# One value visit per head pair and a deeper weight ring in a fused attention, MLP and experts kernel

## The chip, the cores and the metric

The kernel runs on one core of one Trainium2 chip, as one launch. The metric is device time in microseconds, the median of three runs; the kernel before takes 1066.63 us (1066.08 to 1066.88). Durations below come from one profiled execution of the same kernel.

## The reference

Three layers follow each other on 1792 tokens (4 batches of 448): attention with a tanh cap on the scores, an MLP with a piecewise quadratic activation, and a layer of eight experts of which each token takes one. All inputs are f32, but for the two matrices of the first MLP, which arrive as f64. In short:

```python
def reference(q, k, v, cap, moe_w_in, moe_w_out, w_gate, w1, w2):
    # attention, 4 batches x 12 heads x 448 x 64
    scores = q @ k.T / sqrt(64)
    scores = cap * tanh(scores / cap)
    attn = exp(scores - max(scores)); attn /= sum(attn) + 1e-9
    x = concat_heads(attn @ v)                      # 1792 x 768
    # first MLP, 768 -> 2048 -> 768
    h = x @ moe_w_in
    g = where(h >= 1, h, where(h <= -1, 0, (h + 1)**2 / 4))
    x = g @ moe_w_out
    # experts, 8 of them, top 1
    e = argmax(x @ w_gate); p = softmax(x @ w_gate)[e]
    out = p * (relu(x @ w1[e]) @ w2[e])             # 768 -> 1024 -> 768
```

## The kernel before

**Arithmetic.** The large products keep f32 accuracy by splitting both operands into a high part that the fast f32 mode of TensorE (fp32r) holds exactly and a low rest. Each product is then three matmuls: high by high, low by high and high by low. The splits of the raw MLP weights are `unit_split` (ScalarE casts the high part, line 1287; VectorE subtracts for the low part, line 965). The products of probabilities with values (line 1133) and the sums of the probabilities (line 1137) are plain f32, which the profile shows as two records for each matmul.

**Attention.** Heads are handled in pairs, six to a batch, 24 in all, numbered g. For a pair, `load` and `load_v` fetch k, q and v, `prep` transposes k and q on TensorE into high and low parts, and `scores(g, c)` makes the transposed scores of a chunk c of keys: chunks 0 to 2 are 128 keys wide, for both heads, as a 128x896 tile whose matmuls use 64 rows of the array each; chunk 3 is the last 64 keys of both heads at once, through the block diagonal tile `kd`, 128x448, on the whole array. ScalarE applies tanh and exp to each chunk, and the result is the tile t of probabilities (tags pe and po for even and odd chunks, three tiles each, all of full size). `values(g, c)` adds the chunk's product with v into a PSUM tile, 64 columns of the array for each head; with chunk 3 go four matmuls for the sums, from chunk 3 and from `ta`, the sum of the other three chunks, made on VectorE. `finish` copies both out, inverts the sums by way of DRAM (den_s) and scales.

**First MLP.** For a batch, `gemm1` makes 16 column blocks of h from 32 units of weights (two units of 384 columns for each block, nine matmuls for each unit) and `gemm2` 6 blocks of y from 24 units of 512. `step(u)` asks for the raw weights of unit u+4 and for the split of unit u+2. Raw weights lie in a ring of three tiles (tag wr). In batch 0 the f64 weights are first converted to f32 and stored in DRAM (wi_s, wo_s); the units of all batches are read from there.

**The order.** Nothing runs where it is written. Every step is recorded with its engine, an estimated cost, its inputs and outputs, and a class `Plan` simulates the five engines and the transfers and emits each engine's instructions in the order of its simulated starts. A step starts when its inputs are done, its engine is free and its tiles have a free place; among several the one recorded earlier goes first, shifted by a table of numbers by name. A transfer is held back while the simulated backlog of the transfers is long. The engines then run these orders strictly. The generators `attn_gen` and `moe1_gen` record the steps: attention of batch b+1 beside the first MLP of batch b, so the attention of batches 1 to 3 lies beside the first MLP of batches 0 to 2. In `attn_gen`, u counts the chunks of a batch, and the values of chunk u - 2 (LAG) are recorded after the scores of chunk u. The experts come last, in an order written by hand.

Of the kernel before, what the change touches and what calls it, by code (L numbers as in the profile page):

```python
# [11 lines left out]
F32 = mybir.dt.float32  # L12
# [9 lines left out]
B, H, S, D = 4, 12, 448, 64  # L22
# [884 lines left out]
def kernel(ctx, tc, q, k, v, cap, w_in, w_out, w_gate, w1, w2, consts, cols, out):  # L907
# [136 lines left out]
    def load(g):  # L1044
        b, pr = divmod(g, NP)
        kq = A([CP, NCH, 4, D], F32, "kq", f"kq{g}", 1)
        for j in range(2):
            for a, i, order in ((k, j, "(c p) d -> p c d"), (q, 2 + j, "(p c) d -> p c d")):
                on, qe = ("ACT", ACT) if g == 0 and i > 1 else ("SP", SP)
                op(on, 630, lambda a=a, i=i, j=j, order=order, qe=qe: qe.dma_start(kq.t[:, :, i], a[b, 2 * pr + j].rearrange(order, c=NCH)),  # L1050
                   wr=[(kq, i)], dma=8 * S * D)
        st[g] = dict(kq=kq)
# [35 lines left out]
    def scores(g, c):  # L1088
# [21 lines left out]
        t = A([128, 2, S], F32, "po" if c % 2 else "pe", f"t{g}_{c}", 3)  # L1110
# [11 lines left out]
    def values(g, c):  # L1122

        s = st[g]
        if c == 0:
            s["pv"] = Sym(PA, [128, 512], F32, "pv", 1, f"pv{g}")
            s["su"] = Sym(PA, [128, 512], F32, "su", 1, f"su{g}")
        pvs, sus, t = s["pv"], s["su"], s["p", c]

        def go():  # L1130
            px = lambda j: t.t[:, j if c < 3 else 0]
            for j in range(2):
                PE.matmul(pvs.t[rows(j), :S], s["vn"][:, c, j], px(j), start=c == 0, stop=c == 3)  # L1133
            if c == 3:
                for n in range(4):
                    j, i = n // 2, n % 2
                    PE.matmul(sus.t[32 * n : 32 * n + 32, :S], one[:, (1 + j) * i], px(j) if i else s["ta"].t[:, j], start=True, stop=True)

        op("PE", 1740 if c == 3 else 870, go, rd=[(t, j) for j in range(2 if c < 3 else 1)] + [(s["vk"], i) for i in range(4)] + [("one", 0)]
           + ([(s["ta"], 0)] if c == 3 else []), wr=[(pvs, 0)] + ([(sus, 0)] if c == 3 else []), duty=0.87)  # L1140
# [28 lines left out]
    def attn_gen(b):  # L1169
# [12 lines left out]
        for u in range(4 * NP + LAG):  # L1182
# [4 lines left out]
            if u >= LAG:  # L1187
                done = b * NP + (u - LAG) // 4
                values(done, (u - LAG) % 4)
# [69 lines left out]
    def unit_load(u):  # L1259
# [6 lines left out]
        r = Sym(MP, [128, 512], F32, "wr", 3, f"wr{u}")  # L1266
# [24 lines left out]
    def step(u):  # L1291
        unit_load(u + 4)
        unit_split(u + 2)
# [3 lines left out]
    def gemm1(b):  # L1297
        u = b * NU
        if b == 0:
            for i in range(4):  # L1300
                unit_load(i)
# [369 lines left out]
```

## Time and profile before

| | |
|---|---|
| median of three runs | 1066.63 us (1066.08 to 1066.88) |
| the profiled execution: time, span | 1065.99 us, 1064.1 us |
| busy TensorE, weight load, VectorE, ScalarE, GpSimd | 95%, 73%, 49%, 49%, 13% |
| TensorE's mean granted clock | 0.985 of full speed |
| value matmuls (line 1133), 384 records | 96.4 us busy, 593 ns mean |
| transfers | 162.56 MB, mean 153 GB/s |

The busy time of a matmul is modelled and overlaps with its neighbours, so a duration of 0.37 us does not mean that the next matmul starts 0.37 us later. What a matmul costs in a stream is read from the distance of the starts. Attention of batch 0 lies between 7 and some 85 us, the first MLP of batch 0 begins at 84 us, and the last value visit of batch 3 is at 586.59 us. The last stretch, from some 760 us on, is the experts.

### The profile page before, as it was taken

The page shows a single profiled execution, that of the slowest core. Times are in us where ns is not written, and L with a number is a line of the kernel's source. Part 1 is how long each engine was busy: PE and PEld are TensorE (multiplying, and loading weights), DVE is VectorE, ACT ScalarE, POOL GpSimd, SP SyncE. Part 2 cuts the span into 40 slices and gives each one's busy share as a digit, 9 for nine tenths or more (in the row PEclk, how much of TensorE's full clock was granted, in tenths as well). Part 3 has the DMA queues.
Part 4 walks back from the last instruction along what each step waited for, and adds up shares of the span by engine and source line. Part 5 has one row for each costly group of instructions (what it writes and reads, how often), then busy time and mean ns, then how long its engine had stood idle before and what let it go on. Part 6 is the DMA issues. An engine that isn't in the chain of part 4 may idle for free. (4 is left out here: it accounts for less than half of the span.)

```text
span 1064.1 us, 17421 instructions
## 1 busy us (share of the span) xinstructions
PE 1010.5 (95%) x5546; PEld 778.6 (73%) x5546; DVE 522.0 (49%) x1054; ACT 525.4 (49%) x872; POOL 134.4 (13%) x199
## 2 busy tenths in 40 slices
PE   6978899999999999999999999999999989999995
PEld 3435677777687767876777888799767858888984
DVE  5878899678476643357653347752541101110110
ACT  5867667648656653557665344452521212222221
POOL 2221011011020101011101002000311111111110
PEclk9988899999999999999999999999999999999998
DMA  7778888888553444254342344772138883211111
GB/s 225 187 209 235 262 248 257 265 262 248 155 118 105 121 104 119 83 118 111 108 126 74 104 127 95 235 234 90 53 122 315 306 291 117 70 41 47 46 46 34
DMA packets 167809, 162.56 MB, mean 153 GB/s; under 512 B 90805, under 2 KB 139437, under 8 KB 167682
## 3 DMA queue, kind: packets, MB, share of 16 engines
q1 hardware_dynamic: 163202, 147.83, 47.3%
q0 software_dynamic: 3408, 13.00, 3.7%
q8 instruction: 56, 0.92, 0.4%
q14 instruction: 71, 0.58, 0.2%
q10 hardware_dynamic: 1072, 0.23, 0.1%
HBM read 190.39 MB, written 24.39 MB: 202 GB/s over the span
## 5 line engine op out<-in xcount | busy, mean ns | idle before, releaser
L965 DVE TENSOR_TENSOR wl<-wr,wh 128x384 fp32r<-128x384 f32 (+1 forms) x224 | 138.6, 622 | 116.9 <-ACT wh L1287 114.2
L1287 ACT CAST wh<-wr 128x384 fp32r<-128x384 f32 (+1 forms) x224 | 123.7, 557 | 118.4 <-PE y L1347 69.3
L1318 PE MATMUL h<-xh,wh 128*128 128x448 f32 x384 | 146.8, 382 | 2.1 <-DVE g L1327 1.9
L1320 PE MATMUL h<-xh,wl 128*128 128x448 f32 x384 | 142.5, 371 | 1.8 <-DVE wl L965 1.8
L1346 PE MATMUL y<-gh,wh 128*128 128x448 f32 x384 | 144.0, 375 | 0.0
L1319 PE MATMUL h<-xl,wh 128*128 128x448 f32 x384 | 141.9, 369 | 0.4 <-DVE xl L965 0.4
L1347 PE MATMUL y<-gl,wh 128*128 128x448 f32 x384 | 140.3, 365 | 0.0
L1348 PE MATMUL y<-gh,wl 128*128 128x448 f32 x384 | 140.3, 365 | 0.0
L1112 ACT ACTIVATE t<-sc,csc 128x896 f32<-128x896 f32 x96 | 86.8, 916 | 30.5 <-PE sc L1106 15.0
L1133 PE MATMUL pv<-t,vn 128*64 128x448 f32 x384 | 96.4, 593 | 5.0 <-DVE ev L1150 3.4
L499 DVE TENSOR_TENSOR hl<-ht,hh 128x512 fp32r<-128x512 f32 x26 | 18.0, 691 | 165.6 <-ACTq L598 159.9
L1318 PEld LDWEIGHTS h<-xh,wh 128*128 128x128 f32 x384 | 72.9, 190 | 32.5 <-issue 13.3
L1113 ACT ACTIVATE t<-t,capx 128x896 f32<-128x896 f32 x96 | 90.7, 954 | 1.8
L1346 PEld LDWEIGHTS y<-gh,wh 128*128 128x128 f32 x384 | 72.1, 188 | 23.2 <-issue 13.9
L1320 PEld LDWEIGHTS h<-xh,wl 128*128 128x128 f32 x384 | 72.9, 190 | 10.1 <-DVE wl L965 3.7
L1319 PEld LDWEIGHTS h<-xl,wh 128*128 128x128 f32 x384 | 73.0, 190 | 6.5 <-DVE xl L965 0.8
L511 PE MATMUL ey<-w2h,hh 128*128 128x384 f32 x208 | 74.5, 358 | 2.4 <-issue 2.4
L1348 PEld LDWEIGHTS y<-gh,wl 128*128 128x128 f32 x384 | 72.1, 188 | 5.9
L1347 PEld LDWEIGHTS y<-gl,wh 128*128 128x128 f32 x384 | 72.2, 188 | 5.3
L512 PE MATMUL ey<-w2l,hh 128*128 128x384 f32 x208 | 69.9, 336 | 0.0
L513 PE MATMUL ey<-w2h,hl 128*128 128x384 f32 x208 | 69.9, 336 | 0.0
L1325 ACT ACTIVATE g<-h,half 128x448 f32<-128x448 f32 x64 | 40.5, 635 | 53.5 <-PE h L1320 51.6
(252 smaller groups left out, 1617.0 us busy)
## 6 DMA issues: line engine op xcount, KB each, us to landing
s<-in_moe_w_dram SPq DMA_DIRECT2D x84, 512.0 KB
s<-in_moe_w_dram SPq DMA_DIRECT2D x104, 384.0 KB
wr<-wi_s SPq DMA_DIRECT2D x128, 192.0 KB
wr<-wo_s SPq DMA_DIRECT2D x96, 256.0 KB
raws<-in_moe_w_in_dram SPq DMA_DIRECT2D x12, 768.0 KB
raw<-in_moe_w_out_dram SPq DMA_DIRECT2D x12, 512.0 KB
wo_s<-cv SPq DMA_DIRECT2D x24, 256.0 KB
kq<-in_k_dram SPq DMA_DIRECT2D x48, 112.0 KB
```

The lines of the kernel that those rows point to most:

```text
L511: nc.tensor.matmul(o, hh[:, i], self.w2h[f][:, c], start=f == 0, stop=False)
L965: eng.tensor_sub(out, a, hi.bitcast(F32))
L1112: op("ACT", a_(n * S) + 35, lambda: ACT.activation(t.t[:, :n], pt.t[:, :n, :S], AF.Tanh, scale=csc), rd=[(pt, 0), ("cap", 0)], wr=all_)
L1113: op("ACT", a_(n * S) + 85, lambda: ACT.activation(t.t[:, :n], t.t[:, :n], AF.Exp, scale=capx), wr=all_)
L1133: PE.matmul(pvs.t[rows(j), :S], s["vn"][:, c, j], px(j), start=c == 0, stop=c == 3)
L1287: op("ACT", a_(n), lambda: ACT.copy(hi.t[:, :n], r.t[:, :n]), rd=[(r, 0)], wr=[(hi, 0)])
L1318: PE.matmul(pm.t[:, :S], part_of(hi, a), xh[b].t[:, i], start=i == 0, stop=False)
L1319: PE.matmul(pm.t[:, :S], part_of(hi, a), xl[b].t[:, i], start=False, stop=False)
L1320: PE.matmul(pm.t[:, :S], part_of(lo, a), xh[b].t[:, i], start=False, stop=i == NDC - 1)
L1346: PE.matmul(pm.t[:, :S], part_of(hi, f % 4), gh[b].t[:, f], start=f == 0, stop=False)
L1347: PE.matmul(pm.t[:, :S], part_of(hi, f % 4), gl[b].t[:, f], start=False, stop=False)
L1348: PE.matmul(pm.t[:, :S], part_of(lo, f % 4), gh[b].t[:, f], start=False, stop=f == NFC - 1)
```

## The change

Four things are changed. The probabilities of chunks 0 to 2 share one ring of six full tiles (tag p), and chunk 3 has two tiles of half the size (tag pc). In batches 1 to 3 the values of a pair are recorded once, with all four chunks and the sums, where chunk 3 was recorded before; batch 0 keeps a visit for each chunk. Raw weights of even units lie in three further tiles (tag wr2, in the attention's pool), so that there are six, except in the last batch, where the pool is gone; `step` asks for unit u+6, and `gemm1(0)` begins with six loads. The first pair's two q loads are issued on SP instead of ACT.

```diff
--- before.py
+++ after.py
@@ -1046,8 +1046,7 @@
         kq = A([CP, NCH, 4, D], F32, "kq", f"kq{g}", 1)
         for j in range(2):
             for a, i, order in ((k, j, "(c p) d -> p c d"), (q, 2 + j, "(p c) d -> p c d")):
-                on, qe = ("ACT", ACT) if g == 0 and i > 1 else ("SP", SP)
-                op(on, 630, lambda a=a, i=i, j=j, order=order, qe=qe: qe.dma_start(kq.t[:, :, i], a[b, 2 * pr + j].rearrange(order, c=NCH)),
+                op("SP", 630, lambda a=a, i=i, j=j, order=order: SP.dma_start(kq.t[:, :, i], a[b, 2 * pr + j].rearrange(order, c=NCH)),
                    wr=[(kq, i)], dma=8 * S * D)
         st[g] = dict(kq=kq)
 
@@ -1107,7 +1106,7 @@
 
         op("PE", scc(c), go, rd=[(x, 0) for x in (kh, kl, qh, ql)] + ([("kd", (i, h)) for i in range(2) for h in range(2)] if c == 3 else []),
            wr=[(pt, 0)], duty=0.8)
-        t = A([128, 2, S], F32, "po" if c % 2 else "pe", f"t{g}_{c}", 3)
+        t = A([128, 2, S], F32, "p", f"t{g}_{c}", 6) if c < 3 else A([128, 1, S], F32, "pc", f"t{g}_{c}")
         all_ = [(t, j) for j in range(n)]
         op("ACT", a_(n * S) + 35, lambda: ACT.activation(t.t[:, :n], pt.t[:, :n, :S], AF.Tanh, scale=csc), rd=[(pt, 0), ("cap", 0)], wr=all_)
         op("ACT", a_(n * S) + 85, lambda: ACT.activation(t.t[:, :n], t.t[:, :n], AF.Exp, scale=capx), wr=all_)
@@ -1119,25 +1118,27 @@
             ta = s["ta"]
             op("DVE", d1(2 * S), lambda: DVE.tensor_add(ta.t, ta.t, t.t), rd=all_, wr=[(ta, 0)])
 
-    def values(g, c):
+    def values(g, cs):
 
         s = st[g]
-        if c == 0:
+        if 0 in cs:
             s["pv"] = Sym(PA, [128, 512], F32, "pv", 1, f"pv{g}")
             s["su"] = Sym(PA, [128, 512], F32, "su", 1, f"su{g}")
-        pvs, sus, t = s["pv"], s["su"], s["p", c]
+        pvs, sus = s["pv"], s["su"]
+        ts = {c: s["p", c] for c in cs}
 
         def go():
-            px = lambda j: t.t[:, j if c < 3 else 0]
-            for j in range(2):
-                PE.matmul(pvs.t[rows(j), :S], s["vn"][:, c, j], px(j), start=c == 0, stop=c == 3)
-            if c == 3:
+            px = lambda c, j: ts[c].t[:, j if c < 3 else 0]
+            for c in cs:
+                for j in range(2):
+                    PE.matmul(pvs.t[rows(j), :S], s["vn"][:, c, j], px(c, j), start=c == 0, stop=c == 3)
+            if 3 in cs:
                 for n in range(4):
                     j, i = n // 2, n % 2
-                    PE.matmul(sus.t[32 * n : 32 * n + 32, :S], one[:, (1 + j) * i], px(j) if i else s["ta"].t[:, j], start=True, stop=True)
-
-        op("PE", 1740 if c == 3 else 870, go, rd=[(t, j) for j in range(2 if c < 3 else 1)] + [(s["vk"], i) for i in range(4)] + [("one", 0)]
-           + ([(s["ta"], 0)] if c == 3 else []), wr=[(pvs, 0)] + ([(sus, 0)] if c == 3 else []), duty=0.87)
+                    PE.matmul(sus.t[32 * n : 32 * n + 32, :S], one[:, (1 + j) * i], px(3, j) if i else s["ta"].t[:, j], start=True, stop=True)
+
+        op("PE", 870 * (len(cs) + (3 in cs)), go, rd=[(t, j) for c, t in ts.items() for j in range(2 if c < 3 else 1)] + [(s["vk"], i) for i in range(4)] + [("one", 0)]
+           + ([(s["ta"], 0)] if 3 in cs else []), wr=[(pvs, 0)] + ([(sus, 0)] if 3 in cs else []), duty=0.9)
 
     def finish(g):
         b, pr = divmod(g, NP)
@@ -1186,7 +1187,9 @@
                 yield scc(c)
             if u >= LAG:
                 done = b * NP + (u - LAG) // 4
-                values(done, (u - LAG) % 4)
+                c_ = (u - LAG) % 4
+                if b == 0 or c_ == 3:
+                    values(done, range(4) if b else (c_,))
                 if (u - LAG) % 4 == 3:
                     finish(done)
                     if done + 2 < B * NP:
@@ -1263,7 +1266,7 @@
         n = 384 if i < 2 * NFC else 512
         while b == 0 and words and conv_n[0] <= (i // 2 if i < 2 * NFC else i - NFC):
             conv_one(conv_n[0])
-        r = Sym(MP, [128, 512], F32, "wr", 3, f"wr{u}")
+        r = Sym(MP, [128, 512], F32, "wr", 3, f"wr{u}") if b == B - 1 or u % 2 else A([128, 512], F32, "wr2", f"wr{u}", 3)
         if words:
             src = wi_s[i] if i < 2 * NFC else wo_s[i - 2 * NFC]
             go = lambda: SP.dma_start(r.t[:, :n], src)
@@ -1289,7 +1292,7 @@
         wsp[u] = hi, lo
 
     def step(u):
-        unit_load(u + 4)
+        unit_load(u + 6)
         unit_split(u + 2)
 
     part_of = lambda s, i: s.t[:, i * 128 : i * 128 + 128]
@@ -1297,7 +1300,7 @@
     def gemm1(b):
         u = b * NU
         if b == 0:
-            for i in range(4):
+            for i in range(6):
                 unit_load(i)
             unit_split(0)
             unit_split(1)
```

What this does to the order on TensorE, in the second layer of batch 1's MLP beside the attention of batch 2. y is the MLP's second product, pt the transposes of `prep`, sc the scores, pv the values, su the sums; the first digit of a t is the chunk. Before:

```order
L1133 MATMUL pv_4290<-t_1_4220,vn_99 64x448 x2
L1078 MATMUL pt_1_4321<-ct,kq_4119 128x112 x4
L1103 MATMUL sc_3_4326<-qh_4117,kd 128x448 x2
L1103 MATMUL sc_3_4326<-ql_4131,kd 128x448
L1346 MATMUL y_2_4279<-gh_3138,wh_4200 128x448
...
L1133 MATMUL pv_4290<-t_2_4286,vn_99 64x448 x2
...
L1133 MATMUL pv_4290<-t_3_4342,vn_99 64x448 x2
L1137 MATMUL su_4381<-ta_4232,one 32x448
L1137 MATMUL su_4381<-t_3_4342,one 32x448
```

After, at the same pair (line numbers are now those of the new file):

```order
L1077 MATMUL pt_1_4327<-ct,kq_4127 128x112 x4
L1102 MATMUL sc_3_4336<-qh_4125,kd 128x448 x2
L1102 MATMUL sc_3_4336<-ql_4144,kd 128x448
L1349 MATMUL y_2_4285<-gh_3113,wh_4250 128x448
...
L1134 MATMUL pv_4371<-t_0_4190,vn_99 64x448 x2
L1134 MATMUL pv_4371<-t_1_4224,vn_99 64x448 x2
L1134 MATMUL pv_4371<-t_2_4292,vn_99 64x448 x2
L1134 MATMUL pv_4371<-t_3_4351,vn_99 64x448 x2
L1138 MATMUL su_4380<-ta_4229,one 32x448
L1138 MATMUL su_4380<-t_3_4351,one 32x448
```

The four chunks of values, which stood in four places with GEMM matmuls between them, stand in one, ahead of the sums, and behind 12 GEMM matmuls that follow the last scores.

On SP at the start of the program (kq holds k and q of a pair, raws the f64 weights, vn the values). Before:

```order
L935 DMA ct<-in_consts_dram 128x393
L1050 DMA kq_106<-in_k_dram 112x4x64 x2
L1017 DMA raws<-in_moe_w_in_dram 128x6x256
L1058 DMA vn_98<-in_v_dram 128x3x64
L1060 DMA vn_98<-in_v_dram 64x64
L1058 DMA vn_98<-in_v_dram 128x3x64
L1060 DMA vn_98<-in_v_dram 64x64
```

After:

```order
L935 DMA ct<-in_consts_dram 128x393
L1049 DMA kq_112<-in_k_dram 112x4x64
L1049 DMA kq_112<-in_q_dram 112x4x64
L1049 DMA kq_112<-in_k_dram 112x4x64
L1049 DMA kq_112<-in_q_dram 112x4x64
L1017 DMA raws<-in_moe_w_in_dram 128x6x256
L1057 DMA vn_98<-in_v_dram 128x3x64
L1059 DMA vn_98<-in_v_dram 64x64
```

The two q loads now stand between and behind the k loads on SP, ahead of the first f64 weights and of v.

On SP near 470 us of the trace of before, where the sums of pair 18 go out to DRAM and come back (es, rt) between weight loads (wr, with the unit's number). Before:

```order
L1158 DMA den_s_57<-es18_4945 4x448
L1058 DMA vn0_98<-in_v_dram 128x3x64
L1060 DMA vn0_98<-in_v_dram 64x64
L1269 DMA wr123_4968<-wi_s_58 128x384
L1159 DMA rt18_4985<-den_s_57 32x4x14
L1269 DMA wr124_5001<-wi_s_58 128x384
L1269 DMA wr125_5006<-wi_s_58 128x384
L1162 DMA den_s_57<-rt18_4985 32x2x14
L1269 DMA wr126_5037<-wi_s_58 128x384
```

After:

```order
L1159 DMA den_s_57<-es18_4842 4x448
L1057 DMA vn0_98<-in_v_dram 128x3x64
L1059 DMA vn0_98<-in_v_dram 64x64
L1384 DMA y_s_60<-yr1_3_4854 112x768
L1160 DMA rt18_4901<-den_s_57 32x4x14
L1272 DMA wr124_4913<-wi_s_58 128x384
L1272 DMA wr125_4964<-wi_s_58 128x384
L1163 DMA den_s_57<-rt18_4901 32x2x14
L1272 DMA wr126_5000<-wi_s_58 128x384
```

Unit 123's load now stands ahead of the pair's v and sums; units 124 and 125 stand behind the fetch of rt in both orders.

## Rows read from the trace of the kernel before

**Rows 1.** Windows: length, busy us (count) by engine, granted clock, DMA share, GB/s.

```profile
69.20:76.03 6.83, 5.49 (x16) 1.73 (x16) 6.76 (x10) 2.56 (x4) 3.32 (x4) 0.50 0.78 229
82.86:89.68 6.82, 6.21 (x18) 3.89 (x19) 6.74 (x12) 5.04 (x8) 1.15 (x1) 0.50 0.67 194
89.68:116.99 27.31, 25.20 (x133) 16.60 (x133) 22.09 (x34) 18.62 (x29) 4.69 (x9) 1.00 0.94 280
116.99:120.40 3.41, 3.41 (x16) 1.22 (x18) 2.92 (x6) 3.41 (x5) 0.00 (x0) 0.50 0.80 245
123.82:127.23 3.41, 3.41 (x11) 3.01 (x10) 2.92 (x6) 1.63 (x3) 0.00 (x0) 0.50 1.02 264
127.23:280.00 152.77, 152.77 (x802) 113.54 (x800) 121.29 (x216) 100.52 (x164) 17.89 (x28) 1.00 0.81 247
127.00:645.00 518.00, 515.17 (x2701) 391.74 (x2700) 311.43 (x581) 313.93 (x525) 53.24 (x88) 1.00 0.53 150
```

**Rows 2.** Waits of TensorE, 127 to 645 us: total, times, longest.

```profile
PE pt L1078 <- DVE kl L965: 1.9, 1, 1.9
```

**Rows 3.** Timeline of TensorE (start, length) around a value visit between GEMM.

```profile
397.13 0.36 PE L1348 MATMUL y<-gh,wl 128*128 128x448 f32 x1
397.42 0.97 PE L1133 MATMUL pv<-t,vn 128*64 128x448 f32 x4
398.32 0.47 PE L1346 MATMUL y<-gh,wh 128*128 128x448 f32 x1
398.63 0.37 PE L1347 MATMUL y<-gl,wh 128*128 128x448 f32 x1
398.84 0.36 PE L1348 MATMUL y<-gh,wl 128*128 128x448 f32 x1
```

**Rows 4.** Timeline of TensorE, a visit of two chunks before the sums.

```profile
149.83 1.72 PE L1133 MATMUL pv<-t,vn 128*64 128x448 f32 x8
151.48 0.56 PE L1137 MATMUL su<-ta,one 128*32 128x448 f32 x1
```

**Rows 5.** Timeline of TensorE, a visit behind scores.

```profile
329.70 0.37 PE L1320 MATMUL h<-xh,wl 128*128 128x448 f32 x1
330.00 0.47 PE L1106 MATMUL sc<-qh,kh 64*128 64x448 f32 x2
330.31 0.37 PE L1106 MATMUL sc<-qh,kl 64*128 64x448 f32 x2
330.51 0.36 PE L1106 MATMUL sc<-ql,kh 64*128 64x448 f32 x2
330.80 0.97 PE L1133 MATMUL pv<-t,vn 128*64 128x448 f32 x4
331.70 0.47 PE L1318 MATMUL h<-xh,wh 128*128 128x448 f32 x1
```

**Rows 6.** Timeline of TensorE, first and last value visit of batches 1 to 3.

```profile
87.79 1.76 PE L1133 MATMUL pv<-t,vn 128*64 128x448 f32 x4
...
586.59 0.97 PE L1133 MATMUL pv<-t,vn 128*64 128x448 f32 x4
```

**Rows 7.** Timeline of all engines, 471 to 480 us, what led to TensorE's wait.

```profile
471.34 0.86 SPq L1269 DMA_DIRECT2D wr<-wi_s  x2
...
476.35 0.18 DVE L1160 TENSOR_TENSOR rt<-rt 32x28 f32<-32x28 f32 x1 [5.21 <-DMA rt<-den_s]
...
477.03 0.51 ACT L1287 CAST wh<-wr 128x384 fp32r<-128x384 f32 x1 [3.73 <-DMA wr<-wi_s]
...
479.83 0.60 PE L1078 MATMUL pt<-ct,kq 112*128 112x112 f32 x4 [1.90 <-DVE kl L965]
```

**Rows 8.** Timeline of all engines, first 7 us.

```profile
1.21 0.95 SPq L1050 DMA_DIRECT2D kq<-in_k_dram  x2
1.22 1.34 ACTq L1050 DMA_DIRECT2D kq<-in_q_dram  x2
...
6.81 1.73 PE L1078 MATMUL pt<-ct,kq 112*128 112x112 f32 x8 [6.81 <-DMA kq<-in_q_dram]
```

## The prediction

> **What bounds the kernel now.** I read the table of stretches first, then who waited for whom on TensorE, then the timeline of single TensorE visits, because the first two say that TensorE sets the pace and only the third says what it spends its time on. From 127 to 645 us TensorE is busy 515.2 of 518.0 us at full clock, while VectorE and ScalarE work 311.4 and 313.9 us of it [rows 1]. Its longest wait there is 1.9 us, once [rows 2]. So in this stretch, in which almost all of batches 1 to 3 of the attention runs beside the first MLP, an instant saved on TensorE is an instant off the run, and anything else is hidden. Before 127 us it is different. TensorE stands at 1.2 GHz in four pieces (6.83, 6.82, 3.41 and 3.41 us), after waits, and the DMA share is 0.94 from 90 to 117 us [rows 1]. There the order of the waits sets the time.
>
> The timeline shows what a visit costs. In a run of GEMM matmuls each starts 0.20 to 0.21 us after the one ahead (398.63 to 398.84) [rows 3]. The value visit at 397.42 starts 0.29 us after the last GEMM matmul, lasts 0.90 us to the start of the next one (398.32), and the second matmul behind it starts 0.31 us after the first [rows 3]. Two value chunks in one visit take 1.65 us (149.83 to 151.48) [rows 4], so the second chunk adds only 0.75 us. A visit is thus paid for by its number as well as by its work.
>
> **The change, part by part.**
>
> *One value visit per pair in batches 1 to 3.* The timeline of before has 68 value visits between 87.79 and 586.59 us [rows 6], for 18 pairs of 4 chunks (72, so four visits hold two). Afterwards there are 18. The matmuls are the same. The step that joins a chunk to the one before it saves 0.90 - 0.75 = 0.15 us [rows 3, 4], and 50 more chunks are joined. Eight of the old visits lie before 127 us and become two. TensorE waits there anyhow, so I count none of those six, and 44 are left: 44 x 0.15 = 6.6 us.
>
> What stands on either side matters too. Where the visit split a run of whole-array work (GEMM, transposes, the last score chunk with its full-height stationary), its removal also takes away the long step in, 0.29 instead of 0.20, and the long second step behind it, 0.31 instead of 0.21: 0.2 us together [rows 3]. Where it stood beside the scores of the other chunks, which use half the rows, this is not saved, since the scores have the same long second step by themselves (330.00 to 330.31, then 0.20) and the step from scores to values is 0.29 like the one from GEMM [rows 5]. In the written order of before, 30 of the 50 visits that go stand between whole-array work; some three of these lie before 127 us. 27 x 0.2 = 5.3 us. Together 11.9 us. The lower bound is the joins alone, 6.6; the upper one all 50 at the full price of 0.15 + 0.2, 17.5. I take 11.9 because each part of it is a difference between neighbouring rows.
>
> The merged visit is a longer block in an in-order queue. Queued behind it are GEMM matmuls and the next scores, for which ScalarE and VectorE wait. Between the last score chunk of a pair and its visit the new order mostly puts 9 to 36 GEMM matmuls (2 to 7 us at 0.2), and the visit begins with the three older chunks (some 2.3 us), while the last chunk needs only its two short activations. So I put no wait there; the bound is 1 us in each of the few visits that stand close behind their last scores, 3 us in all.
>
> *Probabilities in six full and two half tiles.* Before, a probability tile came free chunk by chunk; now three come free at once, after the visit. The new wait is that of ScalarE's tanh for the pair after next, and behind it in ScalarE's queue stand the weight splits. Six full tiles hold two pairs, and in the new order only two score chunks of the next pair run ahead of a visit, so five of the six are in use. I take 0.
>
> *Ring of raw weights.* Loads are asked for six units ahead instead of four, into six tiles instead of three, except in the last batch, which keeps three. What this can give shows at one place. The load of 471.34 lets ScalarE wait 3.73 us until 477.03, and TensorE then stands 1.9 us until 479.83 [rows 2, 7]. Afterwards that unit is asked for earlier against TensorE's position. But VectorE sits until 476.35 behind another transfer, the sums of a pair (5.21 us) [rows 7], and a deeper ring doesn't move that one. So I take 1.0 of the 1.9 us. The bounds are 1.9 saved and, from three more loads of 192 KB early on, some 2 us lost (576 KB at the 280 GB/s of rows 1), if TensorE has to wait for what they push back.
>
> *The first pair's q loads move from ACT's queue to SP's.* Before, two loads are issued on SP by 2.16 us and two on ACT by 2.56, and the first transpose waits for q until 6.81 [rows 8]. Four issues on SP at 0.48 us end at about 3.1, and the f64 weights and v stand 0.9 us later behind them. Against that, k is now complete first, and it is k and its low part that VectorE makes first. Between 1.0 us sooner and 0.9 later; I take 0.
>
> *The order up to 127 us.* The planner places everything anew, so transfers, conversions and the scores of batch 0 shift. About half of each of the four pieces at 1.2 GHz is loss, some 9 us [rows 1]. I take 0, with 5 us either way. That is the largest unknown.
>
> **Sum.** 6.6 + 5.3 + 1.0 = 12.9 us. The profiled execution took 1065.99 us (its span 1064.1 and 1.9 around it), the median of the runs is 0.6 above that. 1066.6 - 12.9 = 1053.7 us. The experts behind 760 us keep their instructions and their order, and I leave their time as it is.
>
> **Rivals.**
>
> *The early clock, either way.* For it: four low pieces in 127 us, each after TensorE had waited. A new order can lose one more long piece or save one. GEMM matmuls step at 0.2 us at 2.4 GHz and nearly twice that at 1.2, so a 6.8 us piece gained or lost, with the wait ahead of it, moves the end by some 5 or 6 us: 1048.7 or 1059.7. Against the worse side: TensorE has the same work to hand in this stretch. The Trainium skill ("TensorE: Matmul & The Clock Gate", What's actually happening) says that the slow state is the default and that activity lifts it. The low pieces here agree with that; by it alone, gathering the values leaves fewer fillers between the waits of batch 1's first scores, which speaks for the slower of the two sides.
>
> *VectorE becomes the bound in batch 1.* From 127 to 280 us it works 121.3 of 152.8 us [rows 1] and it makes low weight halves, conversions and score inputs in order. If its chains can't follow a TensorE that is 2.5% faster, this third of the gain is lost, 3.8 us: 1057.5. Against it stands that a fifth of its time is idle.
>
> *The boundaries cost nothing.* The 0.2 us at each boundary might be taken up elsewhere, if the modelled busy time hides slack. Then only the joins and the ring stay: 1059.0. Against it: the starts of the rows are what is spaced out, not only the ends.
>
> *Slower than before.* One mechanism: the three extra weight loads land among conversion traffic in the stretch from 90 to 117 us, with its DMA share of 0.94 [rows 1], the transfers that batch 0's last outputs need come later, TensorE runs dry and stays at 1.2 GHz. Its 25.2 busy us there would then take up to 25 us more. It decides from 13 us on, that is, when half of this stretch is slow. At three quarters: 1053.7 + 18.5 = 1072. Against it: the planner holds transfers back while the queue is long, and the loads only come earlier, not oftener.
>
> **How the numbers follow.** Forecast 0.60; early clock better 0.11, worse 0.11; VectorE 0.07; joins only 0.05; slower 0.06. The forecast's own range is 1050 to 1057.5 (the bounds of the small terms). The range of 8 in 10 is 1046.5 to 1062.5; it takes in all cases but the slow one and the tails of the early ones. A measurement here can tell 0.2% (2.1 us) from no change. Faster than that: the first five cases less 0.05 for their tails, 0.89. Within it 0.05. Slower 0.06.
>
> **What would show it.** In the new profile: 18 value visits in batches 1 to 3, each 16 matmul records in about 3.2 us, plus 0.9 for the sums; no TensorE wait near 475 us; the stretch in which the MLPs of batches 0 to 2 run shorter by about 12 us with TensorE as full as before; the experts' part as long as before. The forecast is wrong if TensorE has idle time in the middle stretch, if a chunk inside a visit still takes 0.9 us, or if the low clock before 127 us grows or shrinks by more than one piece.

## The result and the profile after

The changed kernel takes 1056.16 us (median of four runs, 1053.10 to 1057.31), the kernel before beside it 1066.36. The ratio is 0.9908, with a 95% interval of 0.9881 to 0.9934. The forecast was 1053.7 us, a ratio of 0.988. So 10.2 us came of 12.9 forecast.

The profiled execution of after took 1056.16 us, its span 1054.3. Two marks cut both traces into comparable stretches: the sums of the eighth pair (the second of batch 1), and the first matmul of batch 3's first GEMM. These are views of the sums (tile `su`; first and last start behind "ns") and of TensorE's timeline (start, length) of before, then of after:

```profile
L1137 PE MATMUL su<-ta,one x4: 539/563/589, 120.3 to 120.7; 128*32 128x448 f32 x4
...
620.11 0.36 PE L1318 MATMUL h<-xh,wh 128*128 128x448 f32 x1
```

```profile
L1138 PE MATMUL su<-ta,one x4: 539/551/563, 123.2 to 123.6; 128*32 128x448 f32 x4
...
610.97 0.36 PE L1321 MATMUL h<-xh,wh 128*128 128x448 f32 x1
```

Between the marks before needs 499.8 us and after 487.8: 12.0 us less. Up to the first mark after is 2.8 us later. From the second mark to the experts it takes 143.9 us instead of 143.1, and the experts 299.5 instead of 300.9. Together -12.0 + 2.8 + 0.8 - 1.4 = -9.8 us, the difference of the spans (1064.1 and 1054.3). The stretch in the middle gave nearly what was forecast; the start gave some of it back.

Part of both numbers is clock. The last of before's four pieces at 1.2 GHz, 123.82 to 127.23 us, lies behind the first mark with TensorE busy all through it [rows 1]; all four of after lie ahead of its mark. Half of these 3.41 us, 1.7, is an estimate of what that piece cost. So some 10.3 of the 12.0 us come from TensorE's work and waits, and ahead of the mark TensorE is busy at 1.2 GHz for 19.7 us in after and 15.1 in before: half of the difference, an estimated 2.3 us, is most of the 2.8 that it is late. In a second trace of the changed kernel (the run "again" below) the marks lie at 121.2 and 610.4 us: there it is 0.9 us late at the first mark and needs 489.2 between the two.

The windows of after that answer to [rows 1]:

```profile
66.27:73.10 6.83, 5.44 (x19) 2.74 (x19) 5.96 (x11) 4.87 (x7) 1.70 (x4) 0.50 0.77 211
79.92:86.75 6.83, 5.03 (x14) 3.80 (x15) 6.74 (x11) 6.55 (x12) 2.53 (x5) 0.50 0.72 219
100.41:107.23 6.82, 5.79 (x16) 4.54 (x16) 2.09 (x3) 3.01 (x5) 0.38 (x1) 0.50 1.07 350
110.64:114.06 3.42, 3.42 (x11) 3.06 (x10) 3.06 (x6) 3.05 (x5) 0.00 (x0) 0.50 1.00 332
127.23:280.00 152.77, 151.95 (x813) 116.60 (x811) 123.41 (x215) 106.24 (x171) 19.30 (x29) 1.00 0.83 250
127.00:645.00 518.00, 514.00 (x2758) 406.38 (x2757) 322.91 (x613) 323.71 (x537) 62.71 (x90) 1.00 0.55 151
```

TensorE starts 2758 matmul records in the stretch from 127 to 645 us instead of 2701, while its busy time is 514.0 instead of 515.2 us. It was full and stays full, and gets further. VectorE works 123.4 of 152.8 us in batch 1, against 121.3, and is not the bound. At 1.2 GHz TensorE stands for 23.9 us before 127 us instead of 20.5, again in four pieces.

Its longest waits from 127 to 645 us, which answer to [rows 2] (total, times, longest):

```profile
PE yr L1378 <- DVE g L1330: 1.0, 1, 1.0
PE h L1321 <- ACT yr L1381: 0.9, 1, 0.9
PE yr L1378 <- ACT yr L1381: 0.8, 1, 0.8
```

The 1.9 us wait of [rows 2] is gone; nothing over 1.0 has taken its place, though these short ones are new. One merged visit in the timeline of after, which answers to [rows 3, 4]:

```profile
401.27 0.37 PE L1351 MATMUL y<-gh,wl 128*128 128x448 f32 x1
401.57 3.23 PE L1134 MATMUL pv<-t,vn 128*64 128x448 f32 x16
404.73 0.56 PE L1138 MATMUL su<-ta,one 128*32 128x448 f32 x1
...
405.62 0.47 PE L1349 MATMUL y<-gh,wh 128*128 128x448 f32 x1
405.93 0.36 PE L1350 MATMUL y<-gl,wh 128*128 128x448 f32 x1
```

From start to start the sixteen values take 3.16 us, which is 0.90 + 3 x 0.75, and the sums 0.89. All 18 visits of batches 1 to 3 (first at 91.16, last at 575.20) take 3.157 or 3.158 us. The steps in and out are the old ones, 0.30 and 0.31 us, paid once a pair.

What is new stands before the first mark. Timeline of after, engines SP (q marks the queue), POOL and PE:

```profile
92.53 1.56 SPq L1059 DMA_DIRECT2D vn<-in_v_dram  x1
94.19 0.54 SPq L1272 DMA_DIRECT2D wr<-wi_s  x1
94.82 0.38 SPq L1049 DMA_DIRECT2D kq<-in_k_dram  x1
95.25 0.61 SPq L1049 DMA_DIRECT2D kq<-in_q_dram  x1
95.96 1.21 SPq L1165 DMA_DIRECT2D x<-den_s  x2
...
99.67 1.13 POOL L1167 TENSOR_TENSOR x<-ev,x 128x448 f32<-128x448 f32 x1 [12.18 <-DMA x<-den_s]
...
101.44 0.74 PE L1321 MATMUL h<-xh,wh 128*128 128x448 f32 x1 [4.75 <-ACT xh L1254]
102.10 0.74 PE L1322 MATMUL h<-xl,wh 128*128 128x448 f32 x1
```

SP takes up the loads of the last x of batch 0 at 95.96, behind v, weights, k and q. POOL waits for x until 99.67, ScalarE and VectorE split it, and the GEMM of batch 0 stands 4.75 us until 101.44; the clock is halved from 100.41, within this wait, to 107.23 (the third window above). Before had no wait over 1.9 us between 84 and 127 us.

### The profile page after: what moved, and what is told of

It reads as the page before. It is cut to its first block, busy times and chain, and to the rows that moved or that the text cites. A ratio compares the mean times of both kernels' runs of the same rounds, so it can differ in the third digit from the quotient of the medians.

```text
span 1054.3 us, 17413 instructions
## 1 busy us (share of the span) xinstructions
PE 999.0 (95%) x5546; PEld 786.1 (75%) x5546; DVE 524.9 (50%) x1054; ACT 527.3 (50%) x872; POOL 139.8 (13%) x199
## 5 line engine op out<-in xcount | busy, mean ns | idle before, releaser
L1111 ACT ACTIVATE t<-sc,csc 128x896 f32<-128x896 f32 x96 | 86.7, 913 | 19.7 <-PE sc L1105 13.4
L1134 PE MATMUL pv<-t,vn 128*64 128x448 f32 x384 | 82.5, 562 | 3.0 <-ACT t L1112 1.1
L479 PE MATMUL ph<-w1h,ex 128*128 128x512 f32 x156 | 63.6, 408 | 1.6 <-issue 1.6
```

The lines of the kernel that those rows point to most:

```text
L1111: op("ACT", a_(n * S) + 35, lambda: ACT.activation(t.t[:, :n], pt.t[:, :n, :S], AF.Tanh, scale=csc), rd=[(pt, 0), ("cap", 0)], wr=all_)
L1134: PE.matmul(pvs.t[rows(j), :S], s["vn"][:, c, j], px(c, j), start=c == 0, stop=c == 3)
```

## The experiments

They ran on three chips, four kernels on each (the table is in this order), on which the kernel before had medians of 1069 to 1071 us and single runs from 1060 to 1079; so each is told by its ratio to the kernel before on the same chip, with its 95% interval. The changed kernel was run again on the last of them; between chips only ratios are compared.

| kernel | median us (runs) | ratio to before |
|---|---|---|
| visits alone | 1068.21 (10) | 0.9979 [0.9951, 1.0006] |
| changed, without ring | 1072.01 (10) | 1.0018 [0.9988, 1.0048] |
| changed, q loads on ACT | 1061.56 (5) | 0.9907 [0.9877, 0.9938] |
| third v buffer, without ring | 1067.18 (10) | 0.9978 [0.9956, 1.0000] |
| ring alone | 1071.57 (11) | 1.0021 [0.9993, 1.0049] |
| two visits a pair | 1064.23 (11) | 0.9957 [0.9928, 0.9986] |
| without ring, x loads on POOL | 1068.21 (11) | 0.9991 [0.9963, 1.0019] |
| changed, x loads on POOL | 1067.17 (11) | 0.9989 [0.9962, 1.0017] |
| changed, again | 1055.44 (5) | 0.9881 [0.9834, 0.9928] |
| ring of five | 1059.26 (9) | 0.9895 [0.9864, 0.9925] |
| merged in batches 2 and 3 alone | 1061.34 (11) | 0.9912 [0.9880, 0.9944] |
| two k/q buffers | 1056.86 (5) | 0.9885 [0.9842, 0.9929] |

**The parts apart.** The merged visits (with their tiles) put alone into the kernel before:

```diff
-                values(done, (u - LAG) % 4)
+                c_ = (u - LAG) % 4
+                if b == 0 or c_ == 3:
+                    values(done, range(4) if b else (c_,))
```

> The kernel before with the merged visits and the six full and two half tiles alone; the ring (three tiles, four units ahead) and the q loads on ACT's queue are those of before. Theory A (the visits are worth their 11.9 us in the stretch from 127 to 645 us, and the 3 us that are lacking are lost before 127 us because the merged visit holds a v buffer until its end, so that v loads and, behind them in SP's queue, the loads for the pair's result go out late): about 1057.5 us, with a TensorE wait for xh near 95 to 100 us as in the changed kernel. Theory B (the early loss comes from the ring's extra weight loads): about 1054.5 us and no such wait.

Both theories fell: the visits alone bring nothing that can be told from zero. The wait for xh before 127 us is there (2.6 us, in the changed kernel 4.8). TensorE's longest wait in the middle stretch of this kernel:

```profile
PE sc L1103 <- ACT t L1112: 5.7, 1, 5.7
```

The changed kernel with the ring of before:

```diff
-        r = Sym(MP, [128, 512], F32, "wr", 3, f"wr{u}") if b == B - 1 or u % 2 else A([128, 512], F32, "wr2", f"wr{u}", 3)
+        r = Sym(MP, [128, 512], F32, "wr", 3, f"wr{u}")
...
-        unit_load(u + 6)
+        unit_load(u + 4)
```

> The changed kernel with the ring of before (three tiles, loads four units ahead); the merged visits and the q loads on SP stay. Theory A (the ring is worth about 1 us, at the wait near 475 us, and has no part in the early loss): about 1057 us, 1056 to 1059, the wait for xh near 96 us still there. Theory B (the extra loads push back v and x loads before 127 us): 1052 to 1054 us, the early wait smaller than 2 us.

Again both missed. The gain is gone, and the same wait stands at the same place. Its timeline, of SP's queue, ScalarE and TensorE:

```profile
469.34 0.32 SPq L1272 DMA_DIRECT2D wr<-wi_s  x1
472.48 1.10 SPq L1165 DMA_DIRECT2D x<-den_s  x2
473.68 8.14 SPq L1272 DMA_DIRECT2D wr<-wi_s  x4
...
474.70 0.51 ACT L1290 CAST wh<-wr 128x384 fp32r<-128x384 f32 x1 [1.47 <-DMA wr<-wi_s]
480.37 0.51 ACT L1290 CAST wh<-wr 128x384 fp32r<-128x384 f32 x1 [5.16 <-DMA wr<-wi_s]
...
482.40 0.92 PE L1102 MATMUL sc<-qh,kd 128*128 128x448 f32 x2 [4.87 <-ACT t L1111]
```

The window behind it, in the columns of [rows 1]:

```profile
482.59:486.01 3.42, 3.42 (x10) 3.02 (x10) 2.65 (x5) 2.87 (x5) 1.49 (x4) 0.50 0.78 83
```

SP stands from 469.66 to 472.48 until the reciprocal sums of a pair have landed, issues their two loads, and only at 473.68 asks for weights. ScalarE waits 5.16 us for them; behind it in its queue is the tanh of the next scores, for which TensorE waits 4.87 us. After that 3.42 us are at half clock. From the sums of the pair before this place to those of the pair behind it, the kernel without ring takes 40.2 us, the visits alone 40.7, the changed kernel 33.5.

SP's stand is in the changed kernel too (466.88 to 469.90 us in its trace), and TensorE does not wait behind it: with the ring ScalarE has weights in hand. Nor is the stand the whole of it without the ring. By the count of three tiles, the cast at 474.70 waits for the load issued at 469.34, ahead of the stand, and the one at 480.37 for that of 473.68, so the loads themselves took 5.4 and 6.7 us from issue to use there.

How much of the lost gain is this place? Between the two marks the kernel without ring takes 496.5 us, 8.7 more than the changed one, of which 6.6 lie here. The visits alone take 503.4, 15.6 more: 7.2 lie here, and 6.4 between the first mark and the sums of the next pair (36.9 us against 30.5), with half clock from 124.1 to 131.0. No run says whether the visits or the early order cause that second loss.

The Trainium skill ("DMA: Bandwidth & Descriptors", Two DMAs through the same engine are not ordered) says that the engine that issues a transfer has to wait for the completion of the one whose bytes it reads, since a shared queue does not order them. The stand of the kernel without ring, from 469.66 to 472.48, agrees: everything behind the x loads in SP's order waits with them.

The q loads of the first pair back on ACT's queue, the rest as changed:

```diff
-                op("SP", 630, lambda a=a, i=i, j=j, order=order: SP.dma_start(...
+                on, qe = ("ACT", ACT) if g == 0 and i > 1 else ("SP", SP)
+                op(on, 630, lambda a=a, i=i, j=j, order=order, qe=qe: qe.dma_start(...
```

> The changed kernel with the first pair's q loads on ACT's queue as before; ring and merged visits stay. Theory A (the q loads on SP bring the first transposes 1.3 us earlier, and this lasts, since the work before 76 us follows in order): about 1057.5 us, the first transpose at 6.8 us instead of 5.5. Theory B (what is won at the start is waited off before 127 us): 1056 us, within 0.1% of the changed kernel.

The first transposes start at 6.50 us, in the changed kernel at 5.46. The ratio, 0.9907, is that of the changed kernel in the result, 0.9908; its second measurement, 0.9881, lies within the same interval. An interval of 0.3% either way can't decide between theories that are 0.1% apart: the 0 of the prediction stands within its bounds, and is not shown.

The ring put alone into the kernel before (the first diff above the other way, without the visits):

> The kernel before with the deeper ring of raw weights alone; values in one visit per chunk, tiles and q loads as before. Theory C (the merged visits and the ring need each other: the visits let TensorE reach the place behind the sums of a pair with fewer weights in hand, where the transfer of the pair's sums holds SP's queue, and the ring gives it three more units there): the ring alone has only the 1.9 us wait near 475 us to give, ratio to the kernel before 0.998 to 1.000. Theory D (the whole gain is the ring's, the merged visits cost nothing and bring nothing): ratio near 0.991, since the changed kernel with q loads as before had 0.9907.

Theory C, with a ratio of 1.0021 just above its 0.998 to 1.000, which the interval reaches into. The ring alone brings nothing either. Here the place near 480 us is held by another engine, as its timeline shows:

```profile
482.97 0.17 DVE L1160 TENSOR_TENSOR rt<-rt 32x28 f32<-32x28 f32 x1 [4.72 <-DMA rt<-den_s]
...
486.44 0.60 PE L1078 MATMUL pt<-ct,kq 112*128 112x112 f32 x4 [1.41 <-DVE kl L965]
```

VectorE sits behind the sums as in [rows 7], and TensorE still waits 1.41 of the 1.9 us. The two parts are worth nothing one by one and 0.9 to 1.2% together.

**Is it SP's order?** The ring of before, but the x loads issued on POOL's queue:

```diff
-            op("SP", SPQ, lambda j=j: SP.dma_start(x.t[rows(j)], den_s[i, 4 + j].unsqueeze(0).to_broadcast([64, S])),
+            op("POOL", PQ, lambda j=j: POOL.dma_start(x.t[rows(j)], den_s[i, 4 + j].unsqueeze(0).to_broadcast([64, S])),
```

> The changed kernel with the ring of before, and the two loads of a pair's reciprocal sums into x issued on POOL's queue instead of SP's. If the weights were late near 475 to 482 us because SP stood in order behind these two loads (2.8 us until the sums had landed, and 1.2 us for issuing them): the TensorE wait of 4.9 us there is gone or below 1.5 us, no half clock at 482 us, and the time is 4 to 7 us below the changed kernel without ring (ratio 0.995 to 0.998 instead of 1.002). If the three tiles or the transfer itself are the limit: the same wait, and the ratio stays at 1.002.

The mechanism held, the time missed. Its timeline at the place:

```profile
472.39 0.33 SPq L1163 DMA_DIRECT2D den_s<-rt  x1
474.33 7.63 SPq L1272 DMA_DIRECT2D wr<-wi_s  x5
...
479.51 0.51 ACT L1290 CAST wh<-wr 128x384 fp32r<-128x384 f32 x1 [1.29 <-DMA wr<-wi_s]
480.28 0.51 ACT L1290 CAST wh<-wr 128x384 fp32r<-128x384 f32 x1 [0.26 <-DMA wr<-wi_s]
...
482.80 0.65 PE L1102 MATMUL sc<-qh,kd 128*128 128x448 f32 x2 [0.28 <-ACT t L1111]
```

With nothing between the sums and the weights, ScalarE waits 1.29 instead of 5.16 us, TensorE 0.28 instead of 4.87, and the pair takes 34.0 us instead of 40.2, with three tiles as before. The ratio, 0.9991, lies above the 0.995 to 0.998 expected, and its interval holds the 1.0018 of the kernel without ring. The edit has a price elsewhere: at the start its trace has a wait of 11.2 us for k (7.7 without the edit) and half clock from 99.5 to 116.6 us, and at the end POOL takes longer to finish, as told below for the changed kernel with the same edit: 18.1 us lie behind TensorE's last matmul instead of 12.9. So at this place the ring's worth is cover for SP's stand; that the whole of its worth is this, the times do not show.

How much cover is needed: five tiles, five units ahead.

```diff
-        ... A([128, 512], F32, "wr2", f"wr{u}", 3)
+        ... A([128, 512], F32, "wr2", f"wr{u}", 2)
...
-        unit_load(u + 6)
+        unit_load(u + 5)
```

> The changed kernel with a ring of five tiles and loads five units ahead. Without the ring TensorE waits 4.9 to 5.7 us near 477 to 482 us, because SP stands for about 4 us at the x loads of a pair with weight loads behind them; a unit of weights lasts TensorE some 2 us there. If it is this cover in time that the ring gives, one more unit takes about half of the wait away: 1 to 4 us are left, without half clock behind them, and the ratio lies between: 0.992 to 0.998. If the first added tile is enough: no wait over 1 us there, ratio 0.989 to 0.993. If all three are needed: wait and half clock as without the ring, ratio 0.999 to 1.003.

No single wait over 0.9 us is left from 127 to 645 us, and the ratio is that of the changed kernel. Two more tiles and one unit more ahead are enough; the sixth tile buys nothing that can be seen. Four tiles were not run.

**The price of a visit.** Two visits of two chunks a pair:

```diff
-                if b == 0 or c_ == 3:
-                    values(done, range(4) if b else (c_,))
+                if b == 0 or c_ % 2:
+                    values(done, range(c_ - 1, c_ + 1) if b else (c_,))
```

> The changed kernel with two visits of two chunks a pair in batches 1 to 3 instead of one of four: 18 visits more. If a visit costs what the timeline shows (0.15 us for the join that is lost, 0.2 us at its ends in some 6 of 10 cases): 18 x 0.15 + 11 x 0.2 = 4.9 us above the changed kernel, 0.46% (ratio 0.995 to 0.996). Theory D (visits bring nothing): the same time as the changed kernel, ratio 0.991.

The ratio, 0.9957, is the one worked out. Its interval holds neither ratio of the changed kernel (0.9908 and 0.9881), though it overlaps the interval of the first. One of its visits:

```profile
402.10 0.37 PE L1351 MATMUL y<-gh,wl 128*128 128x448 f32 x1
402.40 1.72 PE L1134 MATMUL pv<-t,vn 128*64 128x448 f32 x8
404.05 0.60 PE L1077 MATMUL pt<-ct,kq 112*128 112x112 f32 x4
```

1.65 us for two chunks, twice 0.75 and 0.15, and 0.30 into it. But that the ratio fits is in part luck: not all of the distance is price. From the first matmul of batch 0's second GEMM to the second mark it takes 430.6 us, the changed kernel 427.7: 3.0 us for the 14 pairs there, where 14 of 18 times 4.9 make 3.8. Another 4.6 us were lost before, in an early order that is its own. From the sums of the ninth pair to the second mark, where neither trace has half clock, its value records take 2.4 us more from start to start (for joins of 0.15 us some 2.3 are expected), its waits 2.5 less, and everything else 2.7 more: about 0.2 us for each of the 15 pairs.

**The start.** A third v buffer (without the ring, for space):

```diff
-    vns = [ap.tile([128, NCH, 2, D], F32, bufs=1, name=f"vn{i}") for i in range(2)]
+    vns = [ap.tile([128, NCH, 2, D], F32, bufs=1, name=f"vn{i}") for i in range(3)]
...
+                    late_v.append(g + 2)
```

> The changed kernel with a third v buffer, v asked for right behind k and q of the same pair, so that no v load waits for a merged visit; for want of space the ring is that of before (three tiles, four units ahead), so it is compared with the changed kernel without the ring. Theory A (a v load held by the merged visit blocks SP's queue and makes the x loads of the last pair of batch 0 late): the TensorE wait of 4.8 us for xh near 96 us goes or falls below 2 us, and the time is 2 to 4 us below that of the changed kernel without the ring, some 1053 to 1055 us. Theory B (the x loads are late because the softmax sums of that pair themselves are late): the same wait and the same time within 1 us.

Not decided by the time: the kernel is 0.4% below the one without ring, but in the traces it stands 3.2 us behind that one at the pair before the place near 480 us, and wins 6.5 us at that place, where the transfers now fall otherwise. At the start the wait for xh is gone and one of 6.5 us for k is there. The one without ring, too, waits for k (7.7 us) and not for xh. So that a v load held by the merged visit is the cause, as I had it, isn't borne out.

The changed kernel with x loads on POOL's queue (the diff as above):

> The changed kernel with those two loads on POOL's queue, ring as changed. The last pair's x loads near 96 us then don't stand behind v, weight and k loads in SP's queue: the TensorE wait of 4.8 us for xh near 96 us shrinks by the 2 to 5 us that they stood there, and the time is 1 to 4 us below the changed kernel (ratio 0.987 to 0.990). If the loads themselves are slower from POOL (its issue took 1.0 to 2.4 us for the table's transfers against 0.5 on SP), or the sums are what is late: no gain, ratio 0.990 to 0.993.

A miss: 0.9989. The wait for xh went and a worse one came, in its trace from 84 to 127 us:

```profile
PE pt L1077 <- DMA kq<-in_k_dram: 10.8, 1, 10.8
```

But this wait is not what makes the kernel slower. It passes the first mark at 121.5 us, 1.6 ahead of the first trace of the changed kernel, and the second at 613.3, 2.3 behind. Of the 9.7 us between the two spans most lies at the very end. The last transfer on POOL and the packets of its queue, of the changed kernel and of this one (from the timeline and the page):

```profile
1042.71 1.01 POOL L519 DMA_INDIRECT out_dram<-yo,ida  x1 [10.35 <-POOLq L598]
q0 software_dynamic: 3408, 13.00, 3.8%
```

```profile
1046.04 1.01 POOL L519 DMA_INDIRECT out_dram<-yo,ida  x1 [10.32 <-POOLq L598]
q0 software_dynamic: 5712, 18.50, 5.6%
```

The spans end at 1054.3 and 1064.0, so 11.6 us follow in the one and 17.9 in the other. In this trace 19.2 us lie behind TensorE's last matmul, in that of the other kernel with x loads on POOL 18.1, in the twelve others 12.8 to 13.3. The instruction that differs most is POOL's closing drain, 4.80 us in the changed kernel and 8.65 and 8.74 in these two, whose POOL queue carried 5712 packets instead of 3408. Why more packets make it longer, no run shows. Some 5 to 6 us, 0.5 to 0.6%, are thus the edit's price at the end, and neither expectation had it. Without it the ratios would be about 0.993 here and 0.994 without the ring, by estimate.

Merged visits in batches 2 and 3 alone, and the changed kernel again:

```diff
-                if b == 0 or c_ == 3:
-                    values(done, range(4) if b else (c_,))
+                if b < 2 or c_ == 3:
+                    values(done, range(4) if b > 1 else (c_,))
```

> The changed kernel with merged visits in batches 2 and 3 alone; batches 0 and 1 have a visit per chunk. By the price of a visit: 18 visits more, of which 6 fall before 127 us; 12 x 0.15 + 7 x 0.2 = 3.2 to 4.9 us above the changed kernel, ratio 0.994 to 0.996. If it is the merged visits before 127 us that cost the 3.5 us which the changed kernel loses there, these come back: TensorE's wait for xh near 96 us is below 2 us, and the ratio is 0.990 to 0.992.

> The changed kernel once more, beside the three below. Ratio to the kernel before 0.988 to 0.994. If what it loses before 127 us follows from its order (the x loads of the last pair behind v, weight, k and q loads in SP's queue), TensorE waits 3 to 6 us for xh near 96 to 101 us again. If that wait was chance, it is below 2 us or elsewhere. The experts' part (from the first wait behind 755 us to the end, 299.5 us in the first trace) has the same instructions in all kernels; where it differs by more than 2 us, that is no effect of an edit.

The second trace of the changed kernel has its wait again, 5.2 us for xh. Without merged visits before 127 us there is one at the same place with another name:

```profile
102.77 0.98 PE L1077 MATMUL pt<-ct,kq 112*128 112x112 f32 x4 [4.88 <-DMA wr<-wi_s]
```

So the merged visits before 127 us aren't needed for a long wait there. At the second mark this kernel is 2.3 to 2.9 us behind the two traces of the changed one, somewhat under the 3.2 of the price; by the runs it can't be told from it.

Two buffers for raw k and q, and five full tiles of probabilities:

```diff
-        kq = A([CP, NCH, 4, D], F32, "kq", f"kq{g}", 1)
+        kq = A([CP, NCH, 4, D], F32, "kq", f"kq{g}", 2)
...
-        t = A([128, 2, S], F32, "p", f"t{g}_{c}", 6) if c < 3 else A([128, 1, S], F32, "pc", f"t{g}_{c}")
+        t = A([128, 2, S], F32, "p", f"t{g}_{c}", 5) if c < 3 else A([128, 1, S], F32, "pc", f"t{g}_{c}")
```

> The changed kernel with two buffers for raw k and q, and, for want of space, five full tiles of probabilities. If the loads of k and q, which wait until the transposes of the pair before have read the one buffer, are what makes batch 0's and batch 1's first transposes late: 1 to 4 us below the changed kernel, ratio 0.987 to 0.990. If the transfers before 117 us as a whole set the pace (DMA share 0.8 to 0.95 there): the same time as the changed kernel. If six full tiles were needed: TensorE waits for tanh in the middle stretch, ratio above 0.993.

The window of the first 120 us, of this kernel and of the changed one:

```profile
0.00:120.00 120.00, 97.29 (x510) 53.41 (x512) 87.83 (x139) 83.93 (x114) 27.93 (x58) 0.93 0.80 227
```

```profile
0.00:120.00 120.00, 93.35 (x481) 51.24 (x481) 86.27 (x134) 82.74 (x110) 21.78 (x54) 0.90 0.79 223
```

TensorE gets 29 records further by then, and the longest wait from 84 to 127 us is 1.6 us. It passes the first mark 4.6 and 2.7 us ahead of the two traces of the changed kernel, but the second only 1.4 and 0.8, and the experts begin at 752.1 us against 754.8 and 754.0. The runs don't show it: 0.9885 and 0.9881 have intervals that cover each other. So it is the best candidate, and not shown to be faster. No wait for tanh is among the longest of its middle stretch (none is over 1.5 us), so five full tiles are enough, which the prediction had read from the order.

## Why the prediction was right, and where it was not

*The visits' price was right*, 0.15 us for a join and about 0.2 for a boundary. Summed from start to start between the marks, the value records take 50.5 us instead of 57.2: 6.7 less, for 6.6 forecast. For the boundaries take the stretch from the sums of the ninth pair to the second mark (468.6 us before, 457.3 after), in which neither kernel has half clock: of the 11.3 us less, 6.4 are value records, 1.8 are nine GEMM matmuls that after does ahead of it, the waits grew by 1.2, and 4.3 are left; 5.3 had been forecast for the boundaries of all pairs. So the price is read from the rows twice, but the total owes something to chance: 12.0 us came in the middle for 12.9 forecast, with some 1.7 of it clock.

But these gains are only there while no wait takes their place. "So I put no wait there; the bound is 1 us in each of the few visits" is true of the kernel with its ring. Without it the merged visits lead to a wait of 4.9 to 5.7 us with 3.4 us at half clock behind it, which takes back 6.6 to 7.2 us; by the runs nothing is left of the gain.

*The ring was mis-sized: the step "So I take 1.0 of the 1.9 us".* I took its worth from the wait that before shows [rows 7]. That wait is VectorE's, and the ring alone hardly moves it (1.41 us left, ratio 1.0021), as the prediction said of "the sums of a pair" and then did not follow. What the ring gives is cover for a wait that before doesn't have and the merged visits bring: by the runs 0.7% (0.9979 without and 0.9907 with it, the q loads on ACT in both), 8 us, or 1.1% with the q loads on SP (1.0018 and 0.9908, not run beside each other), of which the traces show 6.6 to 7.2 us at the one place. Both edits came in one change, so the sum stayed right although its split was not. That is luck: the term that was put at 1.0 us for another wait is what the 11.9 hung on.

*The early order, taken as 0 with 5 either way*, cost 2.8 us by the first mark, with 6.8 us more of low clock ahead of it (3.4 more up to 127 us); in the second trace of the changed kernel 0.9. Against the forecast the middle lacks 0.9 us, the start 2.8, batch 3's MLP 0.8, and the experts gave 1.4: 3.1 us between the profiled executions, 2.7 between the medians. In the first trace the early order is the term that was off most, inside its bounds. The sentence on the Trainium skill ("TensorE: Matmul & The Clock Gate", What's actually happening) leant to the slower side, and this side came, at no more than half the 5 to 6 us that were worked out for it; the third piece of half clock begins within the wait that ended at 101.44.

*The rivals.* VectorE did not become the bound. The slower rival's mechanism, weight loads in the crowded stretch from 90 to 117 us, did not decide: without the ring's loads TensorE waits there too, 7.7 us for k. (Three quarters of its 25.2 us are 18.9, where the prediction has 18.5.) What before does at a boundary, 0.29 instead of 0.20 us, is in keeping with the Trainium skill ("TensorEngine Tiling (Array Packing)", Key Properties), by which a change of tiling mode drains the array; it names no price, and the rows give 0.09 on the way in and 0.10 behind.

*Left open*: what sets the long waits between 84 and 108 us. Their names change with the edit (xh 4.8 and 5.2 us, k 6.5 to 11.2, weights 4.9, k's low part 4.1 with the ring alone), and neither the v buffer nor the queue of the x loads nor the merged visits took them away. They shrank below 2 us with two buffers for k and q, in one trace. Open too is how much of each kernel's time is its early order: most kernels have a single trace.

## To carry to other kernels

A visit that leaves whole-array work has a price at each end and at each join; count it from start to start in the timeline and it adds up over a hundred visits. Two edits that are each worth nothing alone can be worth 1% together, when the first makes the bound engine fast enough to meet a stall that the second covers; so try the pair before dropping either. Where one queue issues both a transfer that waits for another to land and the loads of the bound engine, look at what stands behind the waiting one. Before such a transfer moves to another queue, look at the end of the program too: on POOL's queue it cost 5 to 6 us there.

## What was not expected

The experts' part has the same 1747 matmul records in all these kernels, and yet its length differs by 10 us between single traces. Windows from the experts' start to the end, of the changed kernel without ring and of the one with x loads on POOL:

```profile
765.40:1061.30 295.90, 277.09 (x1747) 230.34 (x1744) 51.45 (x177) 67.70 (x122) 39.70 (x41) 0.99 0.38 130
```

```profile
757.93:1064.00 306.07, 278.88 (x1747) 232.18 (x1745) 51.18 (x177) 67.89 (x122) 39.73 (x41) 0.97 0.37 126
```

Of these 10.2 us, 6.3 lie behind the last matmul and are the price of the POOL queue told above, so the expectation that a difference here is no effect of an edit was wrong for this kernel. The rest is spread between single traces. From the first of the 1747 records to the end of the last, the fourteen traces take from 283.3 us (without ring) to 291.9 (q loads on ACT), and much of that goes with the clock: the first has no piece at 1.2 GHz there, the second 13.7 us of it, and those with one piece of 3.4 us take 286.9 to 288.1. It does not explain all: two others without such a piece take 285.8 and 287.1. A single end time of this kernel thus can't tell an edit of 0.5%; the marks inside the trace, with the clock between them, tell more.
